# Half-row transposes, shared banks for sinks, urgent copies and one more Strassen pair in an attention kernel with two layers behind it

## Chip, cores and metric

The kernel runs on one core of one Trainium2 chip. The metric is the device time of an execution in microseconds (us); the median of 3 runs counts.

## What is computed

Attention over 2 batches of 8 heads, 768 positions and 64 dimensions, in which a query sees the first 4 keys (the sinks) and the last 128 positions; then two feed-forward layers on the 1536 tokens of 512 features, each of two matrix products (512 to 2048 and back) with an elementwise gate between them. Inputs are float32.

```python
scores = scale * np.matmul(q, k.transpose(0, 1, 3, 2))
keep = (pos[None, :] < n_sink) | ((rel >= 0) & (rel < window))   # rel = query - key
scores = np.where(keep, scores, -1000000000.0)
a = np.exp(scores - max); a = a / (sum + 1e-09)
x = np.matmul(a, v)                       # then (B, S, H * D) -> (1536, 512)
h = x @ w_in                              # layer 1, and the same for layer 2
g = h if h >= 1 else 0 if h <= -1 else (h + 1)**2 / 4      # layer 1
g = h * clip(h + 3, 0, 6) / 6                              # layer 2
x = g @ w_out
```

## The kernel before, in words

**Attention.** Queries come in blocks of 128 rows, heads in pairs (64 dimensions each, on partitions 0 to 63 and 64 to 127). A *unit* is one block of queries of one pair of heads; 48 units, in 16 pairs (list GROUPS: four pairs of heads for each of the blocks 0 to 3 of batch 0, 4 to 5 of batch 0, 0 to 1 of batch 1 and 2 to 5 of batch 1). For a unit, `score` makes two products on TensorE (L431, one for each head, on 64 rows each and into two banks) against the block of keys before, the sinks' 4 columns and its own block: 128 columns for block 0, 256 for block 1, 260 from block 2 on (KB is 132). VectorE masks and takes the maximum (L444), ScalarE the exponential with its sum (L478), and for two units together `normalise` takes the reciprocal (L455, L456), writes the sink columns, already divided, into `psk` (L459), and multiplies the four pieces of p: three on GpSimd (L469), one on VectorE or ScalarE (L471, L473). `turn` transposes p on TensorE (L514, L515; the identity is the moving operand) into a bank `ps_t`, from which VectorE or ScalarE copies it (L496, L498, in `copy`); `sinks` does the same with `psk` (L523, bank `ps_k`). `mix` multiplies by the values (L553), and the result is split in a high and a low part (L138, L145), the layers' input.

The order on TensorE and on SP, which issues the loads, is that of the program. It goes in *steps*, two units at a time: scores of units g and g+1, transposes of the two units 4 before, their sinks, and the `mix` of the pair that was transposed a step before. The orders of the other engines come from a scheduler; `high_priority` puts an instruction ahead of others that are ready. `Balance` chooses between VectorE and ScalarE by estimated costs. `defer(fn, n)` calls fn n `tick`s later. Four banks (`ps_y`) go round for transposes, sinks and `mix`, four (`ps_h`) for scores. By the table `halves` the first weights of layer 1 are asked for when so many steps are left, and `take` at 24 left begins to unpack them; `fills` puts the layer's first products between the last steps.

**Layers.** Every float32 product is made of three products of rounded parts (high*high, high*low, low*high), 512 columns each; `product` runs over the blocks of 128 of the contraction. `h_group(m, f, c)` makes block f of 128 of the 2048 hidden features for chunk c of 512 tokens (12 products), `y_group` adds its share of the output (12 products). In the first phase all of chunk 0 is finished, and chunks 1 and 2 leave their hidden blocks in HBM (`spill`); the second phase fetches them and runs `y_group` for them. From pair `PLAIN[m]` of hidden blocks on, `paired` replaces the four groups of chunks 1 and 2 for two blocks (48 products) by Strassen's scheme in Winograd's form: 7 products of half the contraction with 6 products each. It needs sums and differences of input blocks, once for a layer (`combine_x`: four tiles t1 to t4, each rounded and with a remainder), and of weights, for each pair (`combine`). Before, PLAIN is (2, 1).

## Time and profile before

| | |
|---|---|
| median of 3 runs | 607.46 us (606.96 to 608.94) |
| profiled execution | 608.58 us, its span 606.8 us |
| TensorE busy | 593.3 us, 98% of the span |
| VectorE, ScalarE, GpSimd busy | 469.4, 392.3, 107.6 us |
| granted TensorE clock | 0.999 of full speed |

Attention fills the span up to 104 us (the layers' first products stand between its last steps), layer 1 goes on to 351, layer 2 to 603. PE is TensorE, PEld its loading of weights, DVE VectorE, ACT ScalarE, POOL GpSimd, SP the engine that issues loads. Products are pipelined: one lasts longer than the distance to the next, so the pace is read from the starts or from a count over a stretch, not from a product's length. A product of two float32 operands leaves two records, a transpose one.

### The profile page before, as it was taken

The numbers are of one execution on the slowest core, as the hardware profiler recorded it, in microseconds if no ns is written. First come the engines' busy times: TensorE is split into PE (matmuls) and PEld (weight loads), VectorE is DVE, ScalarE is ACT, GpSimd is POOL, SyncE is SP. The second block draws the span as 40 slices with busy tenths as digits, with TensorE's granted clock in tenths as the row PEclk, the third lists the DMA queues.
The fourth block names the chain that finished last, engine by engine and source line by source line (L and its number), as shares of the span: only waits on it lengthen the run. The fifth ranks groups of instructions, "written<-read, shape, count | busy, mean of one in ns | idle before, by whom it ended". The sixth has DMA issues, their size and how long they took to land.

```text
span 606.8 us, 8278 instructions
## 1 busy us (share of the span) xinstructions
PE 593.3 (98%) x2898; PEld 474.8 (78%) x2898; DVE 469.4 (77%) x860; ACT 392.3 (65%) x702; POOL 107.6 (18%) x155
## 2 busy tenths in 40 slices
PE   6999899999999999999999999999999999999997
PEld 4666666877788888888888888888888888888885
DVE  5887898799887879476798859988788875666652
ACT  5978888478557576576788667565656545455442
POOL 7776751200111101110000000111011110000000
PEclk9999999999999999999999999999999999999999
DMA  6457402974567586767466205385768554964203
GB/s 191 156 162 249 133 23 73 324 263 157 187 181 231 183 229 176 215 191 260 174 231 220 70 1 172 140 242 180 232 161 244 141 177 134 324 247 139 105 1 139
DMA packets 40986, 107.06 MB, mean 176 GB/s; under 512 B 3440, under 2 KB 13424, under 8 KB 40944
## 3 DMA queue, kind: packets, MB, share of 16 engines
q1 hardware_dynamic: 29488, 72.05, 37.1%
q0 software_dynamic: 11024, 34.08, 18.3%
q8 instruction: 23, 0.38, 0.3%
q10 hardware_dynamic: 432, 0.40, 0.2%
q14 instruction: 19, 0.16, 0.1%
HBM read 69.29 MB, written 35.13 MB: 172 GB/s over the span
## 4 chain that ended last, share of the span: by engine, by line
PE 81%; DVE 7%; ACT 5%; DMA 3%; issue 2%; POOL 1%; ACTq 0%; POOLq 0%; DVEq 0%; SPq 0%
PE ps_y L883 41%; PE ps_h L687 34%; ACT p L478 3%; PE ps_v L553 3%; PE ps_s L431 2%; DMA raw0o<-moe_w_out_dram 1%; DVE p L444 1%; DMA wo_d<-w 1%; DVE w L224 1%; POOL p L469 1%; ACT w L198 1%; PE ps_t L514 1%; DMA kraw<-k_dram 1%; PE ps_t L515 1%; ACT pt L496 1%
## 5 line engine op out<-in xcount | busy, mean ns | idle before, releaser
L883 PE MATMUL ps_y<-gh,wo 128*128 128x512 f32 x768 | 241.7, 389 | 0.0
L883 PEld LDWEIGHTS ps_y<-gh,wo 128*128 128x128 f32 x768 | 144.2, 188 | 29.8
L883 PE MATMUL ps_y<-gl,wo 128*128 128x512 f32 x384 | 149.6, 390 | 0.4 <-DVE gl L145 0.4
L687 PE MATMUL ps_h<-xh,wi 128*128 128x512 f32 x456 | 147.8, 390 | 0.0
L687 PEld LDWEIGHTS ps_h<-xh,wi 128*128 128x128 f32 x456 | 85.6, 188 | 19.6 <-issue 1.6
L687 PE MATMUL ps_h<-xl,wi 128*128 128x512 f32 x228 | 88.8, 390 | 0.0
L883 PEld LDWEIGHTS ps_y<-gl,wo 128*128 128x128 f32 x384 | 72.1, 188 | 16.3 <-DVE gl L145 1.2
L469 POOL TENSOR_SCALAR p<-p,sm 128x260 f32<-128x260 f32 (+2 forms) x68 | 58.3, 874 | 29.5 <-DVE psk L459 19.3
L138 ACT ACTIVATE gh<-r 128x512 fp32r<-128x512 f32 x64 | 40.2, 630 | 27.6 <-PE ps_y L883 27.5
L687 PE MATMUL ps_h<-xt,st 128*128 128x512 f32 x234 | 57.6, 390 | 0.3 <-DVE hq L806 0.3
L145 DVE TENSOR_TENSOR gl<-r,gh 128x512 fp32r<-128x512 f32 x64 | 43.8, 688 | 16.6 <-ACT gh L138 16.3
L478 ACT ACTIVATE p<-p,nm 128x260 f32<-128x260 f32 (+2 forms) x96 | 46.3, 483 | 15.8 <-DVE nm L444 15.5
L687 PEld LDWEIGHTS ps_h<-xt,st 128*128 128x128 f32 x234 | 43.8, 188 | 9.8 <-DVE hq L806 0.7
L687 PEld LDWEIGHTS ps_h<-xl,wi 128*128 128x128 f32 x228 | 42.8, 188 | 9.1 <-DVE xl L145 0.3
L702 POOL DMA_DIRECT2D h_d<-hq x32 | 17.4, 544 | 131.8 <-ACT hq L138 70.2
L444 DVE CUSTOM_DVE_ANT_0 p<-ps_s,mask 128x260 f32<-128x260 f32 (+2 forms) x96 | 34.8, 394 | 6.1 <-PE ps_s L431 6.0
L667 ACT ACTIVATE r<-hq,half 128x512 f32<-128x512 f32 x32 | 22.8, 723 | 24.6 <-DVE gl L145 18.7
L272 POOL DMA_DIRECT2D wo_d<-w x16 | 8.6, 537 | 157.7 <-DVE w L224 157.6
L668 DVE SCALAR_TENSOR_TENSOR r<-r,hq 128x512 f32<-128x512 f32 x32 | 21.8, 691 | 18.6 <-ACT r L667 18.5
L431 PE MATMUL ps_s<-kraw,qraw 64*128 64x260 f32 (+2 forms) x192 | 31.6, 416 | 4.5 <-DMA kraw<-k_dram 4.3
L806 DVE TENSOR_TENSOR hq<-ps_h,p 128x512 f32<-128x512 f32 x39 | 26.8, 687 | 12.0 <-PE ps_h L687 11.9
L431 PEld LDWEIGHTS ps_s<-kraw,qraw 64*128 64x128 f32 x192 | 19.8, 197 | 14.3 <-DMA kraw<-k_dram 5.0
(107 smaller groups left out, 937.0 us busy)
## 6 DMA issues: line engine op xcount, KB each, us to landing
h_d<-hq POOLq DMA_DIRECT2D x32, 512.0 KB, 6.2
hq<-h_d SPq DMA_DIRECT2D x32, 512.0 KB, 5.5
wo_d<-w POOLq DMA_DIRECT2D x16, 512.0 KB, 7.3
raw1i<-moe_w_in_dram SPq DMA_DIRECT2D x8, 1024.0 KB, 6.3
wr<-wo_d SPq DMA_DIRECT2D x16, 512.0 KB, 5.1
raw1o<-moe_w_out_dram SPq DMA_DIRECT2D x8, 1024.0 KB, 6.0
raw0i<-moe_w_in_dram SPq DMA_DIRECT2D x7, 1024.0 KB, 6.3
raw0o<-moe_w_out_dram SPq DMA_DIRECT2D x7, 1024.0 KB, 5.8
```

Of the source, the lines that this page charges most:

```text
L138: nc.scalar.activation(out=dst, in_=src, func=AF.Copy)
L145: nc.vector.tensor_tensor(out=dst, in0=src, in1=f32(hi), op=ALU.subtract)
L431: nc.tensor.matmul(banks[e], tq[rows, u * P:(u + 1) * P], tk[rows, c0:c0 + w], start=True, stop=True)
L444: nc.vector.tensor_tensor_reduce(out=p[:, e, :], in0=banks[e], in1=masks[min(i, 2)], scale=-SCALE, scalar=BIG, op0=ALU.add, op1=ALU.min, a ...
L469: nc.gpsimd.tensor_scalar_mul(out=px, in0=px, scalar1=r)
L478: nc.scalar.activation(out=p[:, e, :], in_=p[:, e, :], func=AF.Exp, scale=-1.0, bias=nm[:, v + e:v + e + 1], accum_out=sm[:, v + e:v + e + 1],
L553: nc.tensor.matmul(ps[e * D:(e + 1) * D, u0 * P:u1 * P], l, r, start=n == 0, stop=n == len(ops[0]) - 1)
L667: nc.scalar.activation(out=r, in_=h, func=AF.Relu, scale=1.0 / 6.0, bias=half)
L668: nc.vector.scalar_tensor_tensor(out=g, in0=r, scalar=1.0, in1=h, op0=ALU.min, op1=ALU.mult)
L687: nc.tensor.matmul(ps, a[:, kc, :], b[kc], start=start and i == 0, stop=i == len(ops) - 1, skip_group_check=not start,)
L806: nc.vector.tensor_tensor(out=dst, in0=src, in1=p1, op=ALU.add)
L883: nc.tensor.matmul(ys[dm], a[:, cs], b, start=fc == 0 and i == 0, stop=last and i == 2)
```

## The change

- `turn` transposes each 128x128 block of p as two halves of 64 rows, each with 64 columns of the identity, into two banks that the two units of a step share; the copies out of them (two for a step, each over both units) come after the second unit's transposes and are urgent.
- `sinks` takes two units of a step together; for pairs four blocks wide the second two units' sinks are put off to the step of the pair's `mix` and go into the same bank as those of the next pair's first two units.
- `normalise` multiplies the two pieces of 128 columns and leaves out the 4 sink columns between them, where there are any.
- The first pair's queries and keys come in three loads instead of two; the weights' first halves are asked for at 56, 50, 44 and 36 steps before the end, and the next weights at 28 (112, 100, 88, 76 and 60 before).
- PLAIN becomes (2, 0): pair 0 of layer 2 goes through `paired` too, with an order of its own for pairs 0 and 1; `combine_x` then comes at the layer's beginning, two of its tiles lie where hidden blocks 2 and 3 will, and the weights' `combine` of pair 0 is put off by 5 ticks. `paired` is written as lists of steps; for the other pairs they are the same steps as before.

```diff
-PLAIN = (2, 1)
+PLAIN = (2, 0)
...
-                defer(lambda: combine(m, p, t32))
+                defer(lambda: combine(m, p, t32), 1 if p else 5)
...
-            parts = [slice(0, P), slice(P, None)] if j == 0 else [slice(None)]
+            parts = [slice(0, P), slice(P, 2 * P), slice(2 * P, None)] if j == 0 else [slice(None)]
...
+                        if w > 2 * P:
+                            px = p4[:, c].rearrange("p (n k) -> p n k", k=KB)[:, :, 0:P]
...
-            ps = bank("ps_t").rearrange("p (e n q) -> p e n q", e=2, n=2)
-            lo = 1 if i == 0 else 0
+            v = u % 2
+            if v == 0:
+                tb[j] = [bank("ps_t").rearrange("p (e b q) -> p e b q", e=2, b=4) for _ in range(2)]
             for e in range(2):
-                if i:
-                    nc.tensor.transpose(ps[:, e, 0, :], p[:, e, 0:P], ident)
-                nc.tensor.transpose(ps[:, e, 1, :], p[:, e, w - P:w], ident)
-            copy(pt[j][0][:, :, u, lo:, :], ps[:, :, lo:, :], 2 * (2 - lo) * P)
-
-        def sinks(j, us):
+                for n in range(0 if i else 1, 2):
+                    for g in range(2):
+                        rows = slice(g * HP, (g + 1) * HP)
+                        cs = slice(n * (w - P), n * (w - P) + P)
+                        nc.tensor.transpose(tb[j][g][:, e, 2 * v + n, :], p[rows, e, cs], ident[rows, rows])
+            if v:
+                lo = 2 * (u - 1) + (1 if i == 1 else 0)
+                blocks = pt[j][0].rearrange("p e u n q -> p e (u n) q")
+                for g, ps in enumerate(tb.pop(j)):
+                    with tc.high_priority(URGENT):
+                        copy(
+                            blocks[:, :, lo:2 * u + 2, g * HP:(g + 1) * HP], ps[:, :, lo - 2 * u + 2:, :],
+                            2 * (2 * u + 2 - lo) * HP,
+                        )
+
+        def sinks(ks):
 
             ps = bank("ps_k").rearrange("p (u q) -> p u q", q=P)
...
+            for n, (j, u) in enumerate(ks):
+                both = psink.pop((j, u // 2))
+                for x in range(2):
+                    nc.tensor.transpose(ps[0:2 * NS, 2 * n + x, :], both[:, 2 * NS * x:2 * NS * (x + 1)], ident)
+            for n, (j, u) in reversed(list(enumerate(ks))):
+                with tc.high_priority(URGENT):
+                    copy(pt[j][1][0:2 * NS, u:u + 2, :], ps[0:2 * NS, 2 * n:2 * n + 2, :], 2 * P)
...
-                if i0 + u > 1:
-                    steps.append(lambda a=(j, (u, u + 1)): sinks(*a))
+                if i0 + u > 1 and (nq < 4 or u + 2 < nq or j == len(pairs) - 1):
+                    ks.append((j, u))
...
+                if GROUPS[pairs[j][0]][3] == 4 and j < len(pairs) - 1:
+                    ks.append((j, 2))
+            if ks:
+                steps.append(lambda ks=ks: sinks(ks))
...
             work = (
-                (1, sub, (0, 1, 0)), (2, sub, (1, 3, 1)), (2, split, (0,)), (3, sub, (3, 3, 0)), (4, split, (1,)),
-                (5, split, (3,)), (7, sub, (2, 2, 3)), (9, split, (2,)),
+                (0, sub, (0, 1, 0)), (1, split, (0,)), (1, sub, (1, 3, 1)), (2, sub, (3, 3, 0)), (2, split, (3,)),
+                (4, split, (1,)), (5, sub, (2, 2, 3)), (6, split, (2,)),
             )
...
+        if p == 0:
+            work = (
+                h(f0), a_low, h(f1), a_high, y(f0), c_first, b_first, (spill_0, c_second), y(f1), b_second, h(f1 + 1),
+                b_third,
+            )
...
-                halves = {112: ("i", 0), 100: ("i", 1), 88: ("o", 0), 76: ("o", 1)}
+                halves = {56: ("i", 0), 50: ("i", 1), 44: ("o", 0), 36: ("o", 1)}
...
-                    if left == 60:
+                    if left == 28:
                         load_w(0, "i", 1)
```

The change moves instructions at three places that matter below. First TensorE in a step of attention, at the second pair of blocks 4 and 5 (`ps_s` scores, `ps_t` transposes, `ps_k` sinks, `ps_v` the product with the values). Before:

```order
L431 MATMUL ps_s<-kraw,qraw 128x260 x4
L514 MATMUL ps_t<-ident,p 128x128
L515 MATMUL ps_t<-ident,p 128x128
...
L523 MATMUL ps_k<-ident,psk 8x128 x2
L553 MATMUL ps_v<-pt,vraw 64x256 x2
L553 MATMUL ps_v<-pt,vraw 64x128 x4
L553 MATMUL ps_v<-pts_128,vs 64x256 x2
```

And now:

```order
L432 MATMUL ps_s<-kraw,qraw 128x260 x4
L521 MATMUL ps_t<-ident,p 128x64 x16
L538 MATMUL ps_k<-ident,psk 8x128 x2
L569 MATMUL ps_v<-pt,vraw 64x256 x2
L569 MATMUL ps_v<-pt,vraw 64x128 x4
L569 MATMUL ps_v<-pts_128,vs 64x256 x2
```

The 8 transposes of 128 columns became 16 of 64; the blocks stand in the same order. In the whole program there are 352 of them for 176, and 12 blocks of sink transposes for 16.

Second, ScalarE's order in the last pair of blocks 0 to 3 and the first two of blocks 4 and 5 (L478, now L481, is the exponential; `pt` and `pts` are the copies of transposes and sinks). Before:

```order
L478 ACTIVATE p,sm<-p,nm 128x260 x4
L496 ACTIVATE pt<-ps_t 128x2x256
L478 ACTIVATE p,sm<-p,nm 128x260 x2
L496 ACTIVATE pt<-ps_t 128x2x256
L478 ACTIVATE p,sm<-p,nm 128x260
L496 ACTIVATE pt<-ps_t 128x2x256
L478 ACTIVATE p,sm<-p,nm 128x260
L496 ACTIVATE pts_129<-ps_k 8x256
```

And now:

```order
L481 ACTIVATE p,sm<-p,nm 128x260 x4
L499 ACTIVATE pt<-ps_t 128x2x4x64
L499 ACTIVATE pts_129<-ps_k 8x256
L499 ACTIVATE pts_128<-ps_k 8x256
L481 ACTIVATE p,sm<-p,nm 128x260 x3
L499 ACTIVATE pt<-ps_t 128x2x4x64 x2
L481 ACTIVATE p,sm<-p,nm 128x260
```

Copies of one step stand side by side, with no exponential between them.

Third, VectorE where layer 2 begins (`xl` remainders of layer 1's output, `x` the differences of input blocks, `xt` the remainders of t1 to t4, `ps_h` the gate, `gl` its remainder). Before:

```order
L145 TENSOR_TENSOR xl_21_3536<-ps_y,xh_21_3534 128x512 x2
L668 SCALAR_TENSOR_TENSOR ps_h<-r,ps_h 128x512
L145 TENSOR_TENSOR gl<-ps_h,gh 128x512
L668 SCALAR_TENSOR_TENSOR ps_h<-r,ps_h 128x512
L145 TENSOR_TENSOR gl<-ps_h,gh 128x512
L757 TENSOR_TENSOR x_0_3512<-x_1_3542,x_0_3512 128x1024
```

And now:

```order
L146 TENSOR_TENSOR xl_21_3718<-ps_y,xh_21_3716 128x512 x2
L785 TENSOR_TENSOR x_0_3694<-x_1_3724,x_0_3694 128x1024
L692 SCALAR_TENSOR_TENSOR ps_h<-r,ps_h 128x512
L785 TENSOR_TENSOR x_1_3724<-x_3_3737,x_1_3724 128x1024
L146 TENSOR_TENSOR xt_3745<-x_0_3694,xt_3745 128x1024
L146 TENSOR_TENSOR gl<-ps_h,gh 128x512
L785 TENSOR_TENSOR x_3_3737<-x_3_3737,x_0_3694 128x1024
L146 TENSOR_TENSOR xt_3745<-x_1_3724,xt_3745 128x1024
L692 SCALAR_TENSOR_TENSOR ps_h<-r,ps_h 128x512
L146 TENSOR_TENSOR xt_3745<-x_3_3737,xt_3745 128x1024
```

The differences and remainders, which came after both gates of the first two groups, now stand among them. On TensorE the layer's first products are now 36 of `h_group` and Strassen's first sum, 12 of `y_group`, then those with t1 and t2.

## Rows read from the trace of the kernel before

**Rows 1.** Head of the page: span; busy us (share) and count of each engine.

```profile
span 606.8 us, 8278 instructions
...
PE 593.3 (98%) x2898; PEld 474.8 (78%) x2898; DVE 469.4 (77%) x860; ACT 392.3 (65%) x702; POOL 107.6 (18%) x155
```

**Rows 2.** Stretches: length; busy (count) of PE, PEld, DVE, ACT, POOL; clock; DMA.

```profile
17.20:43.50 26.30, 25.45 (x198) 17.10 (x198) 22.14 (x99) 21.23 (x73) 19.01 (x22) 1.00 0.46 135
43.50:63.40 19.90, 19.06 (x173) 12.86 (x172) 16.02 (x80) 16.97 (x60) 13.15 (x18) 1.00 0.76 236
63.40:74.50 11.10, 9.36 (x73) 6.24 (x72) 9.16 (x43) 9.63 (x33) 8.26 (x9) 1.00 0.48 145
74.50:104.20 29.70, 29.47 (x207) 19.98 (x206) 27.34 (x81) 26.00 (x67) 10.93 (x11) 1.00 0.15 48
...
154.00:346.00 192.00, 192.00 (x847) 158.95 (x848) 152.73 (x208) 132.74 (x192) 15.85 (x23) 1.00 0.63 197
```

**Rows 3.** Timeline of PE, one step: start us, length us, engine, operation, count.

```profile
40.74 1.15 PE L431 MATMUL ps_s<-kraw,qraw 64*128 64x260 f32 x8
41.82 0.33 PE L514 MATMUL ps_t<-ident,p 128*128 128x128 f32 x1
41.99 0.27 PE L515 MATMUL ps_t<-ident,p 128*128 128x128 f32 x1
42.10 0.27 PE L514 MATMUL ps_t<-ident,p 128*128 128x128 f32 x1
...
43.22 0.38 PE L523 MATMUL ps_k<-ident,psk 128*8 128x128 f32 x2
```

**Rows 4.** Groups by shape: count | busy us, mean ns | idle before.

```profile
L514 PE MATMUL ps_t<-ident,p 128*128 128x128 f32 x80 | 20.3, 288 | 3.1 <-POOL p L469 3.0
...
L515 PEld LDWEIGHTS ps_t<-ident,p 128*128 128x128 f32 x96 | 12.9, 141 | 2.9 <-issue 2.0 <-POOL p L469 0.7
...
L523 PEld LDWEIGHTS ps_k<-ident,psk 128*8 128x8 f32 x32 | 2.5, 87 | 1.1 <-ACT pt L496 0.7
```

**Rows 5.** Groups by shape, multiplies of p.

```profile
L469 POOL TENSOR_SCALAR p<-p,sm 128x260 f32<-128x260 f32 x44 | 41.4, 958 | 24.2 <-DVE psk L459 19.3 <-ACT p L478 4.9
...
L473 DVE TENSOR_SCALAR p<-p,sm 128x260 f32<-128x260 f32 x12 | 6.0, 511 | 0.2
...
L471 ACT ACTIVATE p<-p,sm 128x260 f32<-128x260 f32 x8 | 3.9, 502 | 0.2 <-DVE psk L459 0.2
...
L473 DVE TENSOR_SCALAR p<-p,sm 128x256 f32<-128x256 f32 x5 | 1.8, 367 | 0.1
```

**Rows 6.** Timeline of PE, the first 12 us.

```profile
3.12 0.80 PE L431 MATMUL ps_s<-kraw,qraw 64*128 64x128 f32 x4 [3.12 <-DMA kraw<-k_dram]
5.08 3.51 PE L431 MATMUL ps_s<-kraw,qraw 64*128 64x256 f32 x14 [1.17 <-DMA kraw<-k_dram]
```

**Rows 7.** Timeline of ACT, the first 12 us: third block's first exponential.

```profile
7.91 0.50 ACT L478 ACTIVATE p<-p,nm 128x260 f32<-128x260 f32 x1
```

**Rows 8.** DMA issues of the page: count, KB each, us to landing.

```profile
raw0i<-moe_w_in_dram SPq DMA_DIRECT2D x7, 1024.0 KB, 6.3
```

**Rows 9.** Timeline of PE, layer 2's first product.

```profile
350.99 0.39 PE L687 MATMUL ps_h<-xh,wi 128*128 128x512 f32 x1
```

**Rows 10.** Timeline of ACT, the last copy of layer 2's input.

```profile
354.59 0.74 ACT L891 ACTIVATE x<-ps_y 128x512 f32<-128x512 f32 x1
```

**Rows 11.** Busy time by stretch, layer 2's first 10 us.

```profile
351.00:361.00 10.00, 10.00 (x46) 8.29 (x45) 4.13 (x7) 6.35 (x13) 0.00 (x0) 1.00 0.01 2
```

**Rows 12.** Groups by shape, pieces of layer 2's preparation.

```profile
L138 ACT ACTIVATE xt<-x 128x1024 fp32r<-128x1024 f32 x8 | 8.4, 1056 | 3.4 <-DVE x L757 3.4
...
L668 DVE SCALAR_TENSOR_TENSOR ps_h<-r,ps_h 128x512 f32<-128x512 f32 x16 | 11.1, 691 | 10.2 <-ACT r L667 10.2
...
L757 DVE TENSOR_TENSOR x<-x,x 128x1024 f32<-128x1024 f32 x5 | 6.1, 1219 | 0.0
```

**Rows 13.** Timeline of PE, the worst step: transposes that wait.

```profile
67.07 0.33 PE L514 MATMUL ps_t<-ident,p 128*128 128x128 f32 x1 [0.47 <-POOL p L469]
```

More of the change, by code (lines that the diff above doesn't have):

```diff
@@ L17 @@
 P = 128
+HP = P // 2
 NEG = -1.0e30
@@ L371, in build_fast_attention @@
             at[ci] = col0[-1] + nq * P
-        two = {}
+        two, tb = {}, {}
         qk, vv, probs, psink, pt = {}, {}, {}, {}, {}
@@ L733, in x32 @@
             return x32s["a", i]
+        if m:
+            if ("a", i) not in x32s:
+                x32s["a", i] = st_p[0].tile([P, HK, N], F32, tag=f"hq{i}", name=f"x32_{i}", bufs=1)
+            return x32s["a", i]
         if (m, i // 2) not in x32s:
@@ L810, in add_c @@
             nc.gpsimd.dma_start(out=h_d[m][p][:, 1::2, :], in_=ct, accum_op=ALU.add)
-        h_group(m, f0, 0)
-        tick()
-        turn_weights(m, "i", p + 1)
-        a = bank_h()
-        product(a, part(wi[m, f0], k0), x_tiles(m, 1, k0))
-        put(p1, a)
-        tick()
-        swap = p == PLAIN[m]
-        if swap:
-            h_group(m, f1, 0)
-        else:
-            y_group(m, f0 - 1, 0)
-        tick()
-        product(a, part(wi[m, f0], k1), x_tiles(m, 1, k1), start=False)
@@ L826, in paired @@
-        put(hf0[:, 0], a)
-        if last:
-            fetch(m, 0)
-            load_wo(m, 0)
-            fetch(m, 1)
-            load_wo(m, 1)
-            defer(lambda: split_wo(m, 0), 2)
-        tick()
-        b = bank_h()
-        product(b, s2, t2)
-        plus(hf0[:, 1], b)
-        tick()
-        if swap:
-            y_group(m, f0 - 1, 0)
-        else:
-            h_group(m, f1, 0)
-        tick()
-        spill(m, f0)
-        c = bank_h()
-        product(c, s1, t1)
-        put(ct[:, 1], c)
@@ L847, in paired, with a_low @@
-        tick()
-        turn_weights(m, "o", p + 1)
-        product(b, s3, t3, start=False)
-        plus(hf1[:, 1], b)
-        tick()
-        y_group(m, f0, 0)
-        tick()
-        product(c, s4, x_tiles(m, 2, k1), start=False)
-        put(ct[:, 0], c)
-        if last:
-            start(m, 0)
-            start(m, 1)
-        tick()
-        product(b, part(wi[m, f1], k1), t4, start=False)
-        plus(hf1[:, 0], b)
-        tick()
+        def a_low():
+            a = banks["a"] = bank_h()
+            product(a, part(wi[m, f0], k0), x_tiles(m, 1, k0))
+            put(p1, a)
@@ new lines, in a_high, with b_first, b_second @@
+        def a_high():
+            a = banks["a"]
+            product(a, part(wi[m, f0], k1), x_tiles(m, 1, k1), start=False)
+            put(hf0[:, 0], a)
+            if last:
+                fetch(m, 0)
+                load_wo(m, 0)
+                fetch(m, 1)
+                load_wo(m, 1)
+                defer(lambda: split_wo(m, 0), 2)
+        def b_first():
+            b = banks["b"] = bank_h()
+            product(b, s2, t2)
+            plus(hf0[:, 1], b)
+        def b_second():
+            turn_weights(m, "o", p + 1)
+            b = banks["b"]
+            product(b, s3, t3, start=False)
+            plus(hf1[:, 1], b)
@@ new lines, in b_third, with c_first, c_second, spill_0 @@
+        def b_third():
+            b = banks["b"]
+            product(b, part(wi[m, f1], k1), t4, start=False)
+            plus(hf1[:, 0], b)
+        def c_first():
+            c = banks["c"] = bank_h()
+            product(c, s1, t1)
+            put(ct[:, 1], c)
+        def c_second():
+            c = banks["c"]
+            product(c, s4, x_tiles(m, 2, k1), start=False)
+            put(ct[:, 0], c)
+            if last:
+                start(m, 0)
+                start(m, 1)
+        def spill_0():
+            spill(m, f0)
@@ new lines, in h, with y, turn_in @@
+        def h(f):
+            return lambda: h_group(m, f, 0)
+        def y(f):
+            return lambda: y_group(m, f, 0)
+        def turn_in():
+            turn_weights(m, "i", p + 1)
+        banks = {}
+        if p == 0:
+            work = (
+                h(f0), a_low, h(f1), a_high, y(f0), c_first, b_first, (spill_0, c_second), y(f1), b_second, h(f1 + 1),
+                b_third,
+            )
+        elif p == 1 and PLAIN[m] == 0:
+            work = (
+                (turn_in, a_low), c_first, h(f1), a_high, b_first, (spill_0, c_second), b_second, y(f0), b_third,
+            )
+        elif p == PLAIN[m]:
+            work = (
+                h(f0), (turn_in, a_low), h(f1), a_high, b_first, y(f0 - 1), (spill_0, c_first), b_second, y(f0),
+                c_second, b_third,
+            )
+        else:
+            work = (
+                h(f0), (turn_in, a_low), y(f0 - 1), a_high, b_first, h(f1), (spill_0, c_first), b_second, y(f0),
+                c_second, b_third,
+            )
@@ L863, in paired @@
+        for fns in work:
+            for fn in fns if isinstance(fns, tuple) else (fns,):
+                fn()
+            tick()
         defer(lambda: spill(m, f1), 2)
```

17 lines of the change are left out of this document (10 added, 7 removed).

## The prediction

> **What bounds the kernel now.** First the head of the page: TensorE is busy 98% of a 606.8 us span [rows 1]. The reader is to see that a microsecond counts only if it is taken off TensorE's own work or off one of its waits. Next the table of busy time by stretch [rows 2], which splits the span into two kinds of work. From 104 us on stand the two layers: 847 products of 512 columns in 192.00 us with no idle, 0.2267 us each; only fewer products shorten that. Before 104 us stands attention, where three engines are nearly full at once: from 17.2 to 63.4 us TensorE 44.5 of 46.2 us, VectorE 38.2, ScalarE 38.2. So work taken off TensorE there is paid out only until VectorE and ScalarE end later. Then the timeline of TensorE through one step of attention [rows 3] gives the price of a transpose and of a change between products on 64 rows and on 128, and the groups by shape [rows 4, 5] give the rest.
>
> **Transposes in halves.** There are 96 + 80 transposes of 128x128 [rows 4]; inside a block they start 0.11 us apart (41.99, 42.10) [rows 3], 0.109 for 128 moving columns. The change makes two of each, on rows 0 to 63 and 64 to 127, 64 columns each, into two banks. Do such halves run beside each other? The scores already work like that (two heads on 64 rows each, into two banks): 8 records of 260 columns start at 40.74 and the next transpose at 41.82. One after the other at 0.109 us per 128 columns they would take 8 x 0.22 = 1.77 us; two at once 0.88, and 0.20 is left. So two at once, and a pair of halves costs what 64 columns cost, 0.055 us (estimate; the trace has no 64-column product). Saving 176 x 0.054 = 9.5 us. Worst, the halves run one after the other (0.109 for the two, saving nothing).
>
> What sets 0.109, the loading of weights or the columns? The two transposes of sink columns load 8 columns instead of 128 (87 ns against 141) and still are 0.11 apart (0.38 for two, of which one lasts 0.27) [rows 3, 4]. So the load does not set it here, and the load's own part for 128 columns is about 54 ns, just inside a half's 0.055. The Trainium skill, page "TensorE: Matmul & The Clock Gate", section "LDWEIGHTS (loading the stationary operand)", says against this change that the load's time goes by the columns alone, P/1.2 ns, and that fewer rows make it no shorter: an estimate by it is 107 ns for either half, so a pair would stay where the whole is. No run here shows a load of half the rows in a transpose; the 87 and 141 ns grow by less per column than that rule.
>
> Changing rows: the 0.20 left above and 0.17 instead of 0.11 between the first two transposes (41.82, 41.99) [rows 3] belong to two changes, into the scores and out of them; I take 0.15 us for one. Scores and transposes now have the same rows: 22 of 24 blocks lose one change, 12 blocks of sink transposes and 2 blocks after layer products gain one. Net 8 x 0.15 = 1.2 us. So TensorE's own work in attention falls by 10.7 us.
>
> **What of it is paid out.** From 17.2 to 63.4 us stand 92 of the transposes in 13 blocks, and some 7 of the sink blocks: 92 x 0.054 + (13 - 7) x 0.15 = 5.9 us, floor of TensorE 40.3 us with its waits kept. VectorE and ScalarE have 76.4 us of work on two engines, 38.2 each. How full can they run? From 74.5 to 104.2 they are at 27.34 and 26.00 of 29.70 [rows 2], 89.8% on the mean. At that share 38.2 us need 42.5: they, not TensorE, end last, and I take -3.7 us (bounds -5.9, where TensorE sets the end, and -1.1, at 84.7%, what the stretch after has). From 63.4 to 74.5: 9.40 us at 89.8% is 10.5, -0.6 (0 to -1.7, all its idle). From 74.5 to 104.2 nothing, they are as full as they get (0 to -2).
>
> The copies' number stays (48 of transposes, 16 of sinks), and their urgency only reorders. Their cover is the step between a transpose and the product that uses it; without it see the third rival. The sinks of a pair four blocks wide now wait for the step of the product itself; eight or ten of its products stand ahead of the two that read them, so nothing.
>
> **Sinks left out of the multiplies.** VectorE takes 511 ns for 260 columns and 367 for 256; ScalarE 502 for 260 [rows 5]. The order gives VectorE 22 such multiplies (17 before) and ScalarE 6 (11). If two pieces of 128 cost 367: 22 x 0.367 + 6 x 0.50 = 11.1 against 12 x 0.511 + 5 x 0.367 + 11 x 0.50 = 13.5 us, 2.4 less on two engines, 1.2 each, over 0.898 -1.3. If they cost 511, nothing. Between them, -0.7.
>
> **First loads.** The first scores run at 3.12, the next wait until 5.08 for the rest of the keys [rows 6]. With 128 columns first, issued as early, they run at about 4; ScalarE, whose exponential of the third block stands at 7.91 [rows 7], can then begin the second block, and so the third, 1 us earlier; but the rest of the load is issued one issue later, and where that lands late nothing is won. -0.8 (-1.5 to +0.4). The layers' weights are asked for later, the last half that is needed 20 steps ahead of its use instead of 64; a step is about 0.8 us (99 us of 125 steps), a load of 1 MB lands in 6.3 [rows 8], so 16 us hide it: nothing. The queries and keys that stood behind them in SP's queue are asked for sooner.
>
> **One more pair by Strassen.** 66 products instead of 72: 6 x 0.2267 = -1.36 us [rows 2]. It stands where layer two begins, at 350.99 [rows 9], and needs differences of input blocks whose copies ScalarE ends at 355.33 (354.59 + 0.74) [rows 10]. In these 10 us ScalarE is busy 6.35 and VectorE 4.13 [rows 11]; now four roundings of 1.06 us on the one, four subtractions of 1.22 us and four remainders of the same size on the other fall into the first 20. The one that is due first after its making is t2: VectorE's order puts three subtractions, two remainders and three steps of 0.69 ahead of it [rows 12]. Begun at about 354, t2 is there at 354 + 6 x 1.22 + 3 x 0.69 = 363.4. Its product stands behind 54 others and is due at 350.99 + 54 x 0.2267 = 363.2. So tight; I take 0.3 back: -1.1 (-1.4 to -0.3). The cover is the 30 products of the two first blocks; gone, the whole chain of 9.4 us would stand open.
>
> **Sum.** -3.7 - 0.6 - 0.7 - 0.8 - 1.1 = -6.9 us on the profiled execution: 606.8 to 599.9 span, 608.58 to 601.7 with the 1.8 us around it. That execution stands 1.1 us over the median of the runs shown, 607.46; nothing in the sum depends on that, so the median becomes 600.6. All worst ends give -1.0, all best -13.8 (with -1.3 for the multiplies).
>
> **Rivals.**
> 1. The halves cost as much as the whole: loads or issue set the pace. For: no product under 128 columns is in the trace, and instructions double. Against: the 87 ns loads at the same pace. It leaves -0.8 - 1.1 - 0.7 and 0.2 of the changes of rows, -2.8: 604.7. The rule of the skill named above gives this one.
> 2. VectorE and ScalarE pack tighter, and TensorE's whole 10.7 us is paid out, with 0.8 and 1.1: -12.6, 594.9. For: from 74.5 to 104.2 VectorE alone reaches 92%. Against: the two must reach 95% together (38.2 of 40.3) in the stretch before.
> 3. Slower: the urgent copies hold ScalarE. Both copies of a step now wait for the second unit's transposes, and stand together in ScalarE's queue ahead of exponentials, where one came between them (the order shows it). A transpose waits for GpSimd's 958 ns multiplies [rows 5], 0.47 us a time in the worst step [rows 13]; ScalarE then stands idle, its exponentials come late, and the next multiplies too. Twice 0.47 in each of the 16 full steps is +15; less TensorE's 10.7 and 1.9 it is +2.4: 609.9. It decides from 0.8 us per step on. Against: a copy has the whole next step until it is read, and GpSimd's three multiplies of a step, 2.9 us, fit the forecast's step (42.5 us for 13).
> 4. Strassen stalls layer two: products wait 2 us for the remainders instead of 0.3, +1.7 on the forecast: 602.3. For: t2 above has no slack. Against: the first three products of the stretch's 102 are all that are due so soon.
>
> **How the numbers follow.** Forecast 0.54, at 600.6 with its own range 597 to 604 (0.15 us a step over 24 steps is 3.6 us either way); rival 1 0.13, 2 0.15, 3 0.11, 4 0.07. The range 595.0 to 606.0 leaves out rival 3, half of rival 2 and a little of the tails: 0.8. Within 0.3% of 607.46, about what a measurement of this kernel can tell from no change, is 605.6 to 609.3. Faster: nearly all of the forecast and of 2 and 4, three quarters of 1, together 0.83; same: the rest of 1 and half of 3, 0.09; slower 0.08.
>
> **What would show it.** Right: blocks of 16 halves last about 0.45 us instead of 0.93; no pause between scores and transposes; attention ends near 98 instead of 104.2 with VectorE and ScalarE at 90%; scores waiting for VectorE where transposes waited for GpSimd; layer two with 6 products fewer and under 0.5 us of waits at its start. Wrong: pairs of halves at 0.109 us; ScalarE idle before a copy; an attention that stays at 99 us with TensorE's idle grown by what its work lost.

## The result, and the profile after

The changed kernel takes 611.73 us (median of 6 executions, 611.10 to 613.63) against 607.64 before: a ratio of 1.0063, 95% interval 1.0042 to 1.0085. It is 4 us slower; 6.9 us less was forecast. The profiled execution took 613.63 us, the slowest of the six, so its span is 5.0 us longer than that of [rows 1] where the median is 4.1 longer. One execution each of runs 3, 10 and 11 below lay well above the others of its kernel; medians, ratios and ranges leave it out.

The head of its page: span, and busy us (share) and count of each engine.

```profile
span 611.8 us, 8616 instructions
...
PE 587.9 (96%) x3068; PEld 472.1 (77%) x3068; DVE 472.5 (77%) x868; ACT 392.6 (64%) x703; POOL 110.5 (18%) x156
```

TensorE's busy time fell by 5.4 us, and the span grew by 5.0: about 10 us more of TensorE waiting. Where? The stretches of [rows 2], the last one prolonged to 107.5 because attention ends 3.3 us later (the first layer product behind it starts at 107.53 instead of 104.23; columns as there):

```profile
17.20:43.50 26.30, 22.14 (x228) 14.95 (x226) 20.49 (x94) 20.16 (x70) 17.88 (x21) 1.00 0.30 85
43.50:63.40 19.90, 18.26 (x222) 12.66 (x220) 16.07 (x78) 16.39 (x58) 13.20 (x18) 1.00 0.63 202
63.40:74.50 11.10, 8.32 (x100) 6.03 (x96) 9.98 (x47) 10.03 (x37) 8.01 (x9) 1.00 0.98 344
74.50:107.50 33.00, 29.49 (x258) 19.35 (x258) 26.61 (x83) 27.05 (x68) 12.65 (x12) 1.00 0.15 49
```

From 17.2 to 43.5 us TensorE has 22.14 us of work where it had 25.45, but VectorE and ScalarE are not fuller for it: 20.49 and 20.16 of 26.30, 77 to 78%, where they had 81 to 84%. All three engines are idle more. The table of waits of the same execution, up to attention's end, names what TensorE waits for (us in all, times, longest):

```profile
PE ps_v L569 <- ACT pts L499: 4.0, 4, 2.3
PE ps_s L432 <- DMA kraw<-k_dram: 3.8, 2, 3.0
PE ps_t L521 <- POOL p L472: 2.1, 4, 0.6
PE ps_v L569 <- DVE pts L501: 1.6, 1, 1.6
PE ps_v L569 <- ACT p L481: 1.5, 1, 1.5
PE ps_k L538 <- DVE pt L501: 1.2, 1, 1.2
PE ps_k L538 <- ACT pt L499: 0.9, 3, 0.3
PE ps_t L521 <- ACT pt L499: 0.8, 2, 0.5
```

Value products (ps_v) wait 5.6 us for the copies of the sinks (pts), in five of the seven pairs whose sinks were put off; before, one such wait had 0.2. The transposes of weights and of sinks (ps_t, ps_k) wait 2.9 us for the copies of weights (pt), before 0.2. These are the two lines of the kernel before:

```profile
PE ps_k L523 <- ACT pt L496: 0.2, 1, 0.2
...
PE ps_v L553 <- ACT pts L496: 0.2, 1, 0.2
```

The changed kernel's longest wait for a copy, in the timelines of ScalarE and TensorE (start us, length us, engine, operation, count, idle before):

```profile
85.97 0.50 ACT L474 ACTIVATE p<-p,sm 128x256 f32<-128x256 f32 x1
86.37 1.06 ACT L499 ACTIVATE pt<-ps_t 128x512 f32<-128x512 f32 x2
87.33 0.62 ACT L499 ACTIVATE pts<-ps_k 8x256 f32<-8x256 f32 x2
87.73 0.20 PEld L569 LDWEIGHTS ps_v<-pts,vs 128*64 128x64 f32 x4 [2.52 <-ACT pts L499]
87.74 1.08 PE L569 MATMUL ps_v<-pts,vs 128*64 128x512 f32 x4 [2.28 <-ACT pts L499]
```

The sinks' two copies stand on ScalarE behind exponentials, a multiply and both copies of the weights; TensorE has done the pair's other products and stands.

One more thing in this execution lies outside attention. In layer one TensorE waits 1.86 us for a copy of ScalarE, which itself stood behind a conversion of weights that waited for a store:

```profile
158.45 1.12 ACT L199 ACTIVATE w<-raw0o 128x1024 f32<-128x1024 f32 x1 [4.13 <-DMA wo_d<-w]
...
160.42 0.58 ACT L834 ACTIVATE ct<-ps_h 128x512 f32<-128x512 f32 x1
```

and right after it the granted clock (the third number from the end) halves (to 1.2 GHz) for 3.4 us:

```profile
158.00:161.00 3.00, 1.19 (x6) 0.65 (x4) 1.40 (x3) 2.55 (x3) 0.00 (x0) 1.00 0.03 12
161.00:165.00 4.00, 3.95 (x10) 3.13 (x11) 3.97 (x4) 0.60 (x1) 0.00 (x0) 0.57 0.00 0
165.00:169.00 4.00, 4.00 (x19) 3.25 (x18) 1.84 (x3) 1.60 (x2) 1.06 (x2) 1.00 0.72 168
```

From the 100th to the 500th product of the layers it takes 94.95 us instead of 92.25; the profiled executions of all experiments below take 90.7 to 92.5 there, but for run 14 (93.3), whose profile has such a wait too. The span's 5.0 us are thus 3.3 of attention and 2.7 of this stretch, less 1.0 for the rest, where layer two has fewer products.

### The profile page after: what moved, and what is told of

Its sections match the earlier page's. It is cut to its first block, busy times and chain, and to the rows that moved or that the text cites. A ratio compares the mean times of both kernels' runs of the same rounds, so it can differ in the third digit from the quotient of the medians.

```text
span 611.8 us, 8616 instructions
## 1 busy us (share of the span) xinstructions
PE 587.9 (96%) x3068; PEld 472.1 (77%) x3068; DVE 472.5 (77%) x868; ACT 392.6 (64%) x703; POOL 110.5 (18%) x156
## 4 chain that ended last, share of the span: by engine, by line
PE 82%; ACT 8%; DVE 5%; DMA 3%; issue 1%; POOL 1%; SPq 0%; ACTq 0%; DVEq 0%
PE ps_y L946 42%; PE ps_h L711 37%; ACT p L481 4%; PE ps_v L569 2%; DMA wo_d<-w 1%; ACT pt L499 1%; DVE p L445 1%; PE ps_s L432 1%; DMA vraw<-v_dram 1%; DVE xl L146 1%; POOL p L472 1%; DVE w L214 0%; ACT w L199 0%; DVE w L225 0%; DMA kraw<-k_dram 0%
## 5 line engine op out<-in xcount | busy, mean ns | idle before, releaser
L711 PE MATMUL ps_h<-xh,wi 128*128 128x512 f32 x432 | 140.6, 390 | 0.0
L711 PEld LDWEIGHTS ps_h<-xh,wi 128*128 128x128 f32 x432 | 81.1, 188 | 18.5 <-issue 1.6
L711 PE MATMUL ps_h<-xl,wi 128*128 128x512 f32 x216 | 84.2, 390 | 0.3 <-DVE xl L146 0.3
L472 POOL TENSOR_SCALAR p<-p,sm 128x256 f32<-128x256 f32 (+1 forms) x68 | 60.0, 897 | 29.4 <-DVE sm L457 19.3
L711 PE MATMUL ps_h<-xt,st 128*128 128x512 f32 x252 | 61.8, 389 | 0.0
L481 ACT ACTIVATE p<-p,nm 128x260 f32<-128x260 f32 (+2 forms) x96 | 46.4, 484 | 14.2 <-DVE nm L445 13.4
L711 PEld LDWEIGHTS ps_h<-xt,st 128*128 128x128 f32 x252 | 47.3, 188 | 9.8
L711 PEld LDWEIGHTS ps_h<-xl,wi 128*128 128x128 f32 x216 | 40.6, 188 | 8.9 <-DVE xl L146 0.7
L726 POOL DMA_DIRECT2D h_d<-hq x32 | 17.6, 549 | 118.4 <-ACT xt L139 43.5
L432 PE MATMUL ps_s<-kraw,qraw 64*128 64x260 f32 (+2 forms) x192 | 34.4, 430 | 4.6 <-DMA kraw<-k_dram 3.8
L839 DVE TENSOR_TENSOR hq<-ps_h,p 128x512 f32<-128x512 f32 x42 | 28.8, 687 | 11.6 <-PE ps_h L711 11.5
L139 ACT ACTIVATE wo<-w 128x1024 fp32r<-128x1024 f32 (+1 forms) x17 | 17.2, 1010 | 24.8 <-DVE w L225 24.8
```

Of the source, the lines that this page charges most:

```text
L139: nc.scalar.activation(out=dst, in_=src, func=AF.Copy)
L432: nc.tensor.matmul(banks[e], tq[rows, u * P:(u + 1) * P], tk[rows, c0:c0 + w], start=True, stop=True)
L472: nc.gpsimd.tensor_scalar_mul(out=px, in0=px, scalar1=r)
L481: nc.scalar.activation(out=p[:, e, :], in_=p[:, e, :], func=AF.Exp, scale=-1.0, bias=nm[:, v + e:v + e + 1], accum_out=sm[:, v + e:v + e + 1],
L711: nc.tensor.matmul(ps, a[:, kc, :], b[kc], start=start and i == 0, stop=i == len(ops) - 1, skip_group_check=not start,)
L726: nc.gpsimd.dma_start(out=h_d[m][fc // 2][:, e:e + 2, :], in_=t)
```

## The experiments

Times are medians. Ratios are to the kernel before on the same chip (607.3 to 608.3 there); they differ a little from the ratios of the medians. Differences between two kernels are differences of these ratios times 607.5. The clock is the mean granted clock of an execution.

**1. The third Strassen pair alone.**

```diff
-PLAIN = (2, 1)
+PLAIN = (2, 0)      # and layer two's lists of work, as in the change; nothing else
```

> The kernel before with only the third Strassen pair in layer two (its order of products, its left and right sums); attention, multiplies and loads as before. Theory: this part of the change works by itself, and its products are on TensorE's path, 606.3 us (1.2 under the kernel before), with the 36th layer product at 104.2 us as before. Rival: the pair's new sums delay something of layer two or its new order of deferred work moves the weights' conversion, so that it gains nothing or loses: 607.5 to 609.

606.68 us, 0.9983 (0.9974 to 0.9991): 1.0 us less. The theory holds; this part works.

**2. The sinks in their own step.**

```diff
-                if i0 + u > 1 and (nq < 4 or u + 2 < nq or j == len(pairs) - 1):
+                if i0 + u > 1:
                     ks.append((j, u))
...
-                if GROUPS[pairs[j][0]][3] == 4 and j < len(pairs) - 1:
-                    ks.append((j, 2))
```

> The changed kernel, but each pair of units has its sinks' transposes and copy in its own step again (a bank and a copy for each), none is put off to the step of the value products. Theory A (the late sinks' copies stand in ScalarE's and VectorE's queues behind other work, and the last two value products of a pair wait for them, 5.6 us in five pairs): 606 to 608, with those waits under 0.5 us in all. Rival B (the copies of the transposed weights come only after the second unit, and that is what TensorE waits for; the sinks' waits only pass to them): 610.5 to 612.5, with the waits for the copies of the transposed weights grown by what the sinks' waits lost.

609.42 us, 1.0033 (1.0016 to 1.0049): 1.8 us less than the changed kernel, and no wait for pts over 0.2. The time lies between the two ranges. The waits of the transposes for copies of weights grew, from 2.9 us (those of the sinks' transposes with them) to 5.7, by half of what the sinks' waits lost:

```profile
PE ps_t L521 <- ACT pt L499: 4.1, 6, 0.8
...
PE ps_t L521 <- DVE pt L501: 1.6, 1, 1.6
```

and in the profile the clock is at half for 7 us, from the wait of 1.61 us on that ends at 16.79:

```profile
12.00:16.00 4.00, 2.57 (x23) 1.63 (x23) 2.79 (x15) 2.81 (x10) 2.99 (x4) 1.00 0.52 149
16.00:23.00 7.00, 6.21 (x37) 4.01 (x39) 3.64 (x16) 2.83 (x10) 4.88 (x6) 0.51 0.01 4
23.00:27.00 4.00, 3.29 (x42) 2.39 (x40) 3.97 (x22) 3.16 (x12) 0.14 (x1) 1.00 0.50 150
```

Of twelve executions one had a clock of 1.000, and took 606.76 us; eleven had 0.992 to 0.994, 609.0 to 612.6.

**3. The weights asked for early again.**

```diff
-                halves = {56: ("i", 0), 50: ("i", 1), 44: ("o", 0), 36: ("o", 1)}
+                halves = {112: ("i", 0), 100: ("i", 1), 88: ("o", 0), 76: ("o", 1)}
...
-                    if left == 28:
+                    if left == 60:
```

> The changed kernel, but the first layer's weights are asked for at the steps of before (112, 100, 88, 76 and 60 steps ahead of attention's end). Theory C (the 2 us wait for ScalarE in layer one at 158.8 us, and the 3.4 us at half clock behind it, come from the weights that arrive later): 608 to 609.5, without that wait. Rival: they come from the order of ScalarE's work against a store of weights that lands late, whatever the loads: 611 to 613 with the wait still there. If the early loads cost attention, as the change supposes, its end comes later than 107.5 us by up to 1.

612.23 us, 1.0092 (1.0068 to 1.0115), 1.8 more than the changed kernel by the ratios, but the intervals overlap, and the medians differ by 0.5. Theory C's time falls: the wait in layer one is shorter (0.8), but in the profile, which is of the slowest execution (615.69), attention ends 4.6 us later, more than either said. Value products now wait for a load of values that stands behind the weights (table of waits), and the clock is at half from 70 to 77 and 90 to 94 us. That the later loads help is likely from this line, and not shown by the time alone; run 12 has more on it.

```profile
PE ps_v L569 <- DMA vraw<-v_dram: 2.7, 1, 2.7
```

**4. Whole blocks again.**

```diff
-            if v == 0:
-                tb[j] = [bank("ps_t")... for _ in range(2)]     # 64-row halves, copies if v
+            ps = bank("ps_t").rearrange("p (e n q) -> p e n q", e=2, n=2)
...
+                    nc.tensor.transpose(ps[:, e, n, :], p[:, e, cs], ident)
+            with tc.high_priority(URGENT):
+                copy(pt[j][0][:, :, u, lo:, :], ps[:, :, lo:, :], 2 * (2 - lo) * P)
```

> The changed kernel, but the weights are transposed as whole 128x128 blocks, a bank and an urgent copy for each unit as soon as it is transposed; the rest as in the changed kernel. Theory (TensorE's own work is not what the attention's end hangs on now; halves saved work that turned into waits): 610 to 613. Rival (the halves' saving is on the path, and without it all of it comes back): 617 to 621. Theory B of the second run (copies after the second unit hurt) would put it under the changed kernel, 608 to 610.

608.31 us, 1.0015 (1.0005 to 1.0024): 2.9 less than with halves, with more TensorE work, in the range of theory B. Nothing of the halves' saving is on the path. The late sinks' waits stay: 4.1 us.

**5. One copy to each engine.**

```diff
-                        copy(blocks[...], ps[...], ...)
+                        if g: nc.vector.tensor_copy(out=dst, in_=src)
+                        else: nc.scalar.activation(out=dst, in_=src, func=AF.Copy)
```

> The changed kernel, but of the two copies of a pair of units' transposed weights one is always ScalarE's and the other always VectorE's (the changed kernel gives each to whichever its running sums call less loaded, at times both to ScalarE). Theory B (a bank of transposes stays held because both its copies stand one behind the other in one queue): 608 to 610, with TensorE's waits for the copies of the transposed weights down to under 1 us in attention. Rival (each copy is late by itself, since it comes only when the second unit is transposed and then stands behind exponentials): 611 to 612.5, waits as before it.

610.92 us, 1.0059 (1.0046 to 1.0072), waits for these copies 2.7 us (0.6 of them a value product's) where they were 2.9. Theory B falls; the rival, whose range begins 0.1 higher, is nearer: they are late wherever they run.

**6. Whole blocks and sinks in their own step** (the edits of 2 and 4 together).

> The changed kernel with both undone: whole 128x128 transposes, a bank and an urgent copy per unit, and the sinks in their own step. What is left of the change are the multiplies of 2x128 columns, the copies' urgency, the later loads and the third Strassen pair. Theory (the late sinks and the halves' common copies each cost what their own runs gave back, 2.3 and 3.4 us, and the two add): 605.5 to 606.5. Rival (the two runs gave back the same waits): 607.5 to 608.5.

604.78 us, 0.9959 (0.9946 to 0.9973): **faster than both kernels**, 2.5 us under the kernel before. It came out under the theory's range. Both parts undone give back 6.3 us by the ratios, more than the 1.8 and 2.9 of runs 2 and 4 together: the two losses do not simply add. Its waits up to 105 us:

```profile
PE ps_s L432 <- DMA kraw<-k_dram: 3.8, 2, 3.1
PE ps_t L519 <- POOL p L472: 0.9, 2, 0.5
PE ps_v L560 <- PE ps_k L529: 0.6, 2, 0.4
...
PE ps_k L529 <- ACT pt L499: 0.2, 1, 0.2
PE ps_v L560 <- ACT pts L499: 0.2, 1, 0.2
```

**7. The halves alone**, on the kernel before (the new `turn`, nothing else).

> The kernel before with the halves alone: transposes of 64 rows, two banks for a pair of units, both copied urgently after the second unit; sinks, multiplies, loads and layer two as before. The forecast priced this part at 3.7 us less: 604. Theory (TensorE's saving turns into waits for the copies, which begin half a step later than those of whole blocks): 608 to 610.5, with TensorE's waits for these copies over 2 us where the kernel before has 0.2.

611.45 us, 1.0062 (1.0039 to 1.0085): 3.8 more, where 3.7 less was forecast. Two blocks of transposes in TensorE's timeline, and what ScalarE does meanwhile:

```profile
22.87 0.66 PE L519 MATMUL ps_t<-ident,p 64*128 64x64 f32 x16
23.46 0.38 PE L535 MATMUL ps_k<-ident,psk 128*8 128x128 f32 x2
...
24.98 0.22 PE L519 MATMUL ps_t<-ident,p 64*128 64x64 f32 x1
...
26.41 0.59 PE L519 MATMUL ps_t<-ident,p 64*128 64x64 f32 x11 [0.92 <-ACT pt L497]
```

```profile
23.79 0.51 ACT L479 ACTIVATE p<-p,nm 128x260 f32<-128x260 f32 x1 [1.16 <-DVE nm L445]
...
25.29 0.50 ACT L479 ACTIVATE p<-p,nm 128x260 f32<-128x260 f32 x1
25.69 0.19 ACT L479 ACTIVATION_READ_ACCUMULATOR p<-p,nm 128x1 f32 x1
25.78 0.58 ACT L497 ACTIVATE pt<-ps_t 128x512 f32<-128x512 f32 x1
```

The first block is over at 23.53. Four exponentials come ahead of ScalarE's copy of it, which begins at 25.78. The next block needs both its banks at once: its first half runs at 24.98 into the one, the second half waits for the other until that copy is done. Two copies a block, both only after the second unit, is what lengthens this loop.

**8. Sinks in their own step and one copy to each engine** (the edits of 2 and 5).

> The changed kernel with the sinks in their own step and the two copies of a pair of units always one on ScalarE, one on VectorE. Theory (the 5.7 us of waits for these copies that remained in the second run are both copies in one queue): 605 to 607, the halves gain at last. Rival (they are late wherever they run): 609 to 610, as the second run.

607.45 us, 0.9993 (0.9980 to 1.0005), between the two. The waits for these copies did not shrink (6.0 us against 5.7), so the queue was not it. Executions at a clock of 0.999 or more took 606.0 to 606.6 (4 of 12), those at 0.993 to 0.997 took 606.8 to 608.8.

**9. Whole blocks, both banks of two units copied after the second** (the edit is against run 6).

```diff
-            with tc.high_priority(URGENT):
-                copy(pt[j][0][:, :, u, lo:, :], ps[:, :, lo:, :], 2 * (2 - lo) * P)
+            if v:
+                for x, ps in enumerate(tb.pop(j)):
+                    copy(...)          # unit u - 1 + x, urgent
```

> The kernel of the sixth run (whole 128x128 transposes, sinks in their own step), but the two banks of a pair of units are both copied only when the second unit is transposed, as the halves need it. Theory D (what the halves lose is that both copies begin after the second unit and stand behind the exponentials and maxima of the next scores, while their banks are held): 607 to 609.5, with over 2 us of TensorE's waits for these copies. Rival E (the halves themselves lose it: their blocks are over so early that TensorE pauses and its granted clock falls): 604.5 to 605.5.

606.42 us, 0.9970 (0.9958 to 0.9983): between the two, 0.7 over run 6 by the ratios and 1.6 by the medians. The intervals of the two overlap. Waits of transposes for these copies are 0.6 us, where run 2 has 5.7, although the copies, too, begin only after the second unit: whole blocks of the first unit go into one bank, and the second is wanted half a block later. So theory D, that late copies alone are the loss, falls, though the time is over rival E's range too.

```profile
PE ps_t L521 <- ACT pt L499: 0.6, 1, 0.6
```

All eleven executions have a clock of 0.999 or 1.000.

**10. Halves copied after each unit.**

```diff
-            if v:
-                lo = 2 * (u - 1) + ...            # both units, 2 copies
+            lo = 2 * u + (1 if i == 0 else 0)     # this unit, 2 copies of 256 columns
```

> The changed kernel with the sinks in their own step and the halves' banks copied after each unit, in four copies of 256 columns instead of two of 512, one of each two on ScalarE and one on VectorE. Theory D: the banks come free sooner, TensorE's waits for these copies fall under 3 us and the time to 604 to 606.5, though the two more copies add about 0.5 us of VectorE and ScalarE work to each pair of units. Rival E: 607 to 609, with half-clock stretches in attention as in the second run. Third: VectorE and ScalarE, 80% busy there without it, become the bound: 608 to 611.

655.43 us, 1.0773 (1.0738 to 1.0808): none of the three. My edit made a new wait: the second unit's halves write the banks that the first unit's copies read.

```profile
PE ps_t L521 <- ACT pt L532: 38.3, 23, 2.8
...
PE ps_t L521 <- DVE pt L529: 2.8, 2, 1.4
```

That is 25 waits of 1.6 us each on the mean: so late is a copy here when TensorE waits for it at once. In the profile the clock was at half in eight stretches, 0.961 on the mean. For theory D the run decides nothing.

**11. Run 6 without urgency** (`copy` outside of `high_priority`).

> The kernel of the sixth run without the urgency of the transposes' copies. The forecast gave urgency nothing: 604.3 to 605.3. Rival (urgency keeps the banks moving): 606 to 607.

604.95 us, 0.9945 (0.9925 to 0.9964): no difference from run 6 that the intervals would show. With whole blocks urgency is worth nothing, as forecast; with halves it was not taken away.

**12. The third Strassen pair and the loads** (the change's three parts of the first load and its later steps for the weights, on run 1).

> The kernel of the first run (before with the third Strassen pair) and beside it only the loads: the first keys and queries in three parts, and the first layer's weights asked for 56 to 28 steps ahead of attention's end. Forecast by its terms (0.8 for the loads, 0.7 for the narrower multiplies, which are still missing here): 605.5 to 606.3. Rival (all of the 1.9 between the first and the sixth run is the loads'): 604.5 to 605.2.

606.14 us, 0.9960 (0.9947 to 0.9973). The loads give 1.4 us by the ratios (0.5 by the medians, of different chips). In the profiles attention ends at 103.08 instead of 104.04; the waits for queries and keys are 3.2 us instead of 3.9, and the one of a value product for the values (1.3 us) is gone. On the same chip run 11, which has the narrower multiplies beside it, is 0.9 faster by the ratios, with intervals that overlap.

Open was now whether the halves lose the rest by the clock or by their banks.

**13. Every pair of units transposed twice**, into the same places, so that TensorE's blocks last as long as whole ones (run 2 otherwise).

```diff
             if v:
+                halves(u - 1)
+                halves(u)
```

> The kernel of the second run (halves, sinks in their own step), but TensorE transposes each pair of units twice into the same places, so that its blocks last as long as those of whole transposes; the copies are as in the second run. Theory E (at full clock the halves lose nothing against whole blocks copied in common, 606.4; what they lose beyond it is a TensorE that pauses and is then granted half its clock): 606 to 607, mean granted clock 0.999 or more in most executions, although TensorE does more. Rival (copies and waits of the halves' layout cost it at any clock): 609 to 611.

617.30 us, 1.0155 (1.0138 to 1.0172): 7.4 more than run 2, over the rival too. The clock is better (0.996 to 0.997), and it doesn't help. Transposes wait no less for copies (7.3 us on ScalarE, 2.7 on VectorE), since the wait stands ahead of a block and the longer block comes on top:

```profile
25.33 0.21 PE L524 MATMUL ps_t<-ident,p 64*128 64x64 f32 x1
26.41 0.96 PE L524 MATMUL ps_t<-ident,p 64*128 64x64 f32 x23 [0.86 <-ACT pt L499]
```

So theory E falls as I put it: at a clock as good as this the halves' layout still costs, and whole blocks that take TensorE as long (run 9) have hardly a wait.

**14. Late sinks transposed ahead of the step's transposes.**

```diff
+            if ahead:
+                steps.append(lambda ks=ahead: sinks(ks))
+            for a in turns:
+                steps.append(lambda a=a: turn(*a))
```

> The changed kernel, but the sinks put off to the value products' step are transposed ahead of that step's block of transposes instead of behind it. Theory A (their copies are late because they are handed to the engines right before the products that read them): the last two products of a pair wait under 2 us in all instead of 5.6, time 607.5 to 609.5. Rival (the copies stand in the queues as before whenever their transposes run): 611 to 612.5.

609.45 us, 1.0028 (1.0016 to 1.0040): 2.1 less than the changed kernel, the waits for pts 1.1 us instead of 5.6 (in the fastest execution, which is the profiled one). Theory A holds.

**15. The same with one copy to each engine** (the edit of 5).

> The same with one of the two copies of the transposed weights always on ScalarE and one on VectorE. If all that speaks for the halves is true (a bank fewer in each step, copies in two queues, no late sinks), this keeps TensorE's saving: 602 to 604.5, under the best kernel so far (604.8). Theory E: pauses and half clock remain, 606 to 609.

608.04 us, 1.0001 (0.9989 to 1.0013). Inside theory E's range; the halves don't keep their saving even so: transposes wait 2.5 us for copies, value products 1.6 for pts, and seven of twelve executions have a clock of 0.993 to 0.997 (608.0 to 609.4, the others 606.8 to 607.5).

## Why the prediction was wrong

By the ratios: what is left in run 6 gives 2.5 us, the late sinks cost 3.4 (run 4 against 6) and the halves 2.9 (the changed kernel against run 4). That these make the 3.8 between the kernels proves nothing, since each run differs from the next by one part; taken off in the other order the halves cost 4.5 (run 2 against 6) and the sinks 1.8.

Not all of it is lost in attention. The first layer product behind attention starts, in the kernel before, the changed one and runs 4, 6, 8 and 14, at:

```profile
104.23 0.50 PE L687 MATMUL ps_h<-xh,wi 128*128 128x512 f32 x1
...
107.53 0.50 PE L711 MATMUL ps_h<-xh,wi 128*128 128x512 f32 x1
...
106.23 0.50 PE L702 MATMUL ps_h<-xh,wi 128*128 128x512 f32 x1
...
103.05 0.50 PE L700 MATMUL ps_h<-xh,wi 128*128 128x512 f32 x1
...
103.45 0.50 PE L713 MATMUL ps_h<-xh,wi 128*128 128x512 f32 x1
...
103.09 0.50 PE L715 MATMUL ps_h<-xh,wi 128*128 128x512 f32 x1
```

With whole blocks the late sinks make attention 3.2 us longer (run 4 against 6), as the ratios say. With halves and the sinks mended (runs 8 and 14, profiles of fast executions with full clock in attention) it ends 0.4 us later than in run 6 and at the same time: TensorE's saving is gone there, and little more than that. Where the clock was at half in attention, for 6.8 us in run 2, 3.4 in run 15 and 10.2 in run 7, attention ended 2.5 us later than in run 6, run 6 and the kernel before. From there to the end the third-Strassen kernels with whole blocks take 499.9 to 501.4 us in their profiles, those with halves 500.0 to 504.3; beyond the wait in layer one it is not known why.

- **How fast halves run: right.** 16 of them hold TensorE from 21.88 to the next scores at 22.37, 0.49 us where 0.45 was said and 0.93 was reckoned for a whole block:

```profile
20.90 1.15 PE L432 MATMUL ps_s<-kraw,qraw 64*128 64x260 f32 x8
21.88 0.66 PE L521 MATMUL ps_t<-ident,p 64*128 64x64 f32 x16
22.37 0.44 PE L432 MATMUL ps_s<-kraw,qraw 64*128 64x128 f32 x2
```

 Rival 1 is out. The rule of the Trainium skill ("TensorE: Matmul & The Clock Gate", section "LDWEIGHTS (loading the stationary operand)") is borne out in one part: a load of 64 rows takes 142 ns on the mean, as long as one of 128 rows (141 in [rows 4]), though not the 107 of its formula. But a pair of halves takes 0.06 us, not the 0.107 worked out from it: the two loads of a pair start within 0.01 us of each other.
- **What of it is paid out, -3.7 and -0.6: wrong, and the main error.** The step was that VectorE and ScalarE end last and can be 89.8% busy, so that TensorE's saving is paid out until they are. They stayed at 77 to 82% in the first two stretches; in run 14, at full clock there, at 84 and 79% in the first. Run 7 measures +3.8 for this part; its one execution at a clock of 1.000 took 608.75 us, 1.4 over the kernel before. The sentence that failed is "Their cover is the step between a transpose and the product that uses it": I looked for who reads the copy, and not for who wants the bank that it empties. That is the next block, 1.5 us after the last (23.46 to 24.98 in run 7), with a copy that begins 2.25 us after its block.
- **The sinks' move, 0: wrong,** +1.8 (with halves) to +3.4 (with whole blocks). "Eight or ten of its products stand ahead" counted TensorE's time ahead of the read, about 2 us, and not what stands ahead of the copy in ScalarE's and VectorE's queues; the waits of up to 2.3 us are what is left over. Run 14 shows that the same sinks, handed over earlier, wait 1.1 us in all.
- **Multiplies -0.7: not refuted, but not shown**: 0.9 by the ratios of runs 11 and 12, whose intervals overlap, and in their profiles attention ends at 103.02 and 103.08. Two pieces of 128 on VectorE take 402 ns, between the two bounds of 367 and 511. **Loads -0.8 and 0**: the sum right in sign, 1.4. That the weights' later loads are worth nothing was probably wrong, since values of attention waited behind them (2.7 us in run 3, 1.3 in run 1, none in run 12); no run has them alone on a kernel without the losses. **Strassen -1.1: right**, 1.0. **Urgency 0: right.** These parts together are run 6.
- **The clock stood nowhere in it.** The mean granted clock was under 0.995 in 41 of 70 executions of the kernels with halves (the changed one and runs 2, 3, 5, 7, 8, 14, 15; in run 10 it was in all, in run 13 in none of four); with whole blocks (before and runs 1, 4, 6, 9, 11, 12) it was 0.996 or more in all. In one and the same kernel the lower clock goes with some 1.3 to 2.7 us (runs 2, 7, 8 and 15). So of run 2's 4.5 us over run 6 somewhat over half goes with the clock (by the one execution at full clock), and the rest is there without it. Where in an execution the clock fell is on record for the profiled ones alone.
- **Rival 3** had the sign and the place, both copies of a block that wait for its second unit, but the wrong victim: ScalarE does not stand idle ahead of the copies (0.0 us before 24 of them in the changed kernel), it has exponentials to do first, and TensorE stands.

What stays open: why the clock falls in one execution of a kernel and not in the next, which pauses it takes, and what of the loss in the changed kernel itself is the clock's (its six executions, at 0.994 to 0.999, show no relation to the time). That two banks at once are the reason is read from the timeline of run 7 and from runs 9 and 13 together; a run with a fifth bank for transposes was not made. Nor is it shown that free banks would have paid the saving out: at full clock and without late sinks attention ends between 103.0 and 103.5 us with whole blocks (runs 6, 9, 11, 12) and with halves (8, 14), so the chain of the other engines may set its length there, whatever TensorE saves. The wait in layer one is not in every profile, though the layers' program is the same: the profile of run 14 has it (1.9 us) and those of runs 2 and 5 hardly (0.6 and 0.3).

## What to carry to other kernels

When TensorE gets faster in a loop over a few banks, count how long a bank is held: from its first write, through whatever stands in the copying engine's queue, to the end of the copy. If the next use comes sooner than that, the time saved turns into a wait. When a copy off the path is moved closer to its reader, count what stands ahead of the copy in its own engine's queue, and not only what the reader has to do first. And of a change with many parts, the parts should be run one by one, since here those that gain 2.5 us were hidden by two that lose 6.

## What was not expected of the hardware

Transposes on two halves of the rows run two at once, 0.06 us a pair, with loads of 142 ns each that start within 0.01 us of each other.

How long TensorE pauses did not tell here when its granted clock would fall. Pauses of 1.6 us in attention came with 3.4 us (run 7) and 6.8 us (run 2) at a granted clock of one half; run 7's second stretch at half, 6.8 us from 68.7 on, had no pause of 0.8 us or more in the 40 us before it; and in the changed kernel's attention, pauses of 1.2, 1.6, 1.5 and 2.3 us came with no fall at all.
